# A delta-rule attention with a gated FFN on one core: the outputs' trip through DRAM by pairs of units, and another order of all tasks

## The chip, the cores and the metric

The kernel runs on one core of one Trainium2 chip. The time is the device time of one execution in microseconds (us). A core has five engines that run their own instruction queues in order: TensorE (PE, matrix products; PEld are its weight loads), VectorE (DVE), ScalarE (ACT), GpSimd (POOL) and SyncE (SP). SP computes nothing here: it issues the DMA transfers between DRAM and the core's memory, in the order of its own queue, and the issue of one takes it some 0.4 us. An engine whose next instruction has to wait holds up everything behind it in its queue.

## What is computed

For each of 4 batches and 8 heads, a state of 48 × 48 is carried along 768 tokens. Each token reads the state with its query, and then corrects it along its normalised key. The outputs of all heads, put side by side, are 3,072 rows of 384 features, which go through a gated two-layer network:

```python
for t in range(S):
    kt, vt, bt = (k_n[:, :, t], v[:, :, t], beta[:, :, t, None])
    y[:, :, t] = np.einsum('bhd,bhde->bhe', q[:, :, t], state)
    v_old = np.einsum('bhde,bhd->bhe', state, kt)
    state = state + bt[:, :, :, None] * np.einsum('bhd,bhe->bhde', kt, vt - v_old)
...
x = np.ascontiguousarray(attn_out.transpose(0, 2, 1, 3)).reshape(B * S, H * D)
h = x @ w_in          # 384 x 2048
g = h * np.cos(h)
return (g @ w_out)    # 2048 x 384
```

Everything is float32.

## The kernel before

**Units and pairs.** The 768 tokens are cut into 24 units of 32 tokens; a unit holds all batches and heads. Two units are a pair, and the network works on pairs, 2 × 128 rows each. The work of a unit n, by the names of the tasks in the code:

- `k`, `q`, `v`, from unit 8 on also `blocks`: loads, issued by SP (`load`, L294; `load_blocks`, L314). `turn` and `turn_out` turn keys and queries, on PE and ACT up to unit 7, on DVE from `blocks` afterwards.
- `gram` (PE, L545), `gram_keys` and `gram_queries` (DVE, L556 and L579): products of keys with keys and with queries.
- The triangular system of a pair m is inverted: `gram_put` of both units writes to DRAM (L597), `gram_get` reads it in another layout (L610, L618), `inv` runs column by column (L655, L662), on DVE for pair 0 and on POOL for all others, `put` writes the inverse (L676) and `get` reads it unit by unit (L687, L695).
- The path from unit to unit: `state` (PE, L712) applies the state, `right` (DVE, L727) makes the right-hand side, `solve` (PE, L775) applies the inverse (for units 0 and 1 in two halves, `solve_half` and `between`, L742), `solve_out` (DVE, L785), `update` (PE, L798) and `update_out` (DVE, L806) give the next state, `within` (PE, L815) completes the outputs.

**Outputs to features.** The network needs the outputs with features on the partitions. Units 0 to 3 are turned on PE (`features`, L834) and copied by ACT (`features_out`, L841). From unit 4 on DVE turns them in blocks of 32 × 32 (`within_turn`, L851), `within_put` (L861) writes them to a tile `y_dr` in DRAM, and `features_out`, by `features_move` (L868), reads them back into the pair's tile `x_ffn`. `y_dr` is made per unit, three at a time; its row of 1,536 bytes holds a partition's four batches side by side. The put therefore takes four DMAs a unit, one for each batch's 32 partitions, and the read takes one, in pieces of a whole row.

**Network.** The weights are 28 loads from DRAM (`weights`, L414), each followed by `split` on ACT, `shift` on DVE and `add` on POOL (L437). Pairs 0 and 1 take the first layer in plain form (`hidden`, L883), the others with fewer products (`layer`, L1000; sums of features by `x_sum`, L962). Then come four steps of gating, by turns on ACT and DVE (`turns` L923, `rest` L930, `cos` L939, `gate` L942), and the second layer, `out` (L1025 for pair 0, L1082 after), collected by ACT and DVE (L1119, L1132) and written by `store` (L1143). In a pair's first layer, `layer(p,0,0)` and `layer(p,0,1)` read only the first unit's features; later steps read the second unit's, or the sums.

**Order.** All tasks are registered with their engine and what they depend on, and are then emitted in an order written out by hand: `Order.LINE` (L53), a list of the tasks' numbers. So the order on each engine's queue is fixed, and a task also waits for the data that it uses. The costs and due times given to `add` are not used by this listing. Buffers are few: `x_ffn` has two, `y` one, and the one bank `two` serves `turn`, `gram`, `solve`, `update` and `features` in turn.

Of the kernel before, what the change touches and what calls it, by code (L numbers as in the profile page):

```python
# [10 lines left out]
FP = mybir.dt.float32  # L11
# [5 lines left out]
C = 32  # L17
# [36 lines left out]
0 1 2 3 4 5 6 1767 14 72 10 15 37 73 42 11 43 7 12 1771 16 38 13 75 17 96 39 40 44 45 18 46 20 48 99  # L54
1772 19 79 1775 50 80 76 77 49 97 47 1779 100 78 101 81 131 104 1773 132 1783 105 102 1768 1774 155
1780 106 51 82 52 107 1769 1784 53 134 1776 54 109 55 84 135 111 1781 1787 108 9 1777 1785 110 83
1778 1788 1782 1791 112 56 36 1770 113 22 41 138 1795 21 1789 23 139 24 25 26 136 27 114 1799 1796
28 1792 29 137 30 115 1786 32 186 31 140 1803 33 74 1807 57 1793 141 1794 1800 142 1790 34 35 1804
1797 1808 58 1805 1809 59 116 679 1810 60 61 818 62 1798 1811 1801 210 684 63 680 1815 681 241 64
1819 685 156 117 1802 65 1820 1812 8 66 686 687 67 1823 68 118 1813 689 143 159 187 1824 69 1816  # L60
1827 98 688 1825 119 1831 1817 86 160 161 162 164 682 163 1828 189 690 103 193 190 194 683 1814 85
1806 694 1832 1835 70 1818 691 71 87 88 165 692 1829 695 89 1839 699 166 1830 90 1836 92 133 1843
1821 191 1833 693 696 1837 697 91 700 1840 698 1822 701 192 704 702 93 705 709 703 1826 167 714 710
94 706 1841 719 265 95 1844 711 712 707 1834 243 1838 168 1847 708 715 169 1842 120 1851 195 731 121
196 1845 197 122 747 123 1846 713 1852 716 170 752 717 124 1848 125 244 718 748 735 1853 753 157
1855 211 1856 749 754 127 171 1849 126 1859 720 755 750 1854 757 1850 1857 128 1860 1861 756 129 758
762 732 751 130 763 214 759 760 215 767 296 1863 1864 158 764 216 765 1867 1858 172 145 761 217 1862
173 188 1868 1871 1865 174 721 1869 1866 768 736 766 769 1872 219 770 739 1873 1870 1875 146 772 771
198 247 1876 248 777 1877 778 1874 1878 245 782 779 249 722 773 144 220 218 147 774 723 221 148 269
819 222 725 737 724 780 149 223 268 151 726 822 152 150 175 820 740 823 176 727 270 775 781 320 783  # L70
741 298 776 224 212 177 728 153 178 729 743 784 733 785 246 787 786 179 788 351 299 790 180 182 821
793 183 794 791 154 744 181 225 792 746 796 184 798 250 200 789 730 799 242 251 800 252 213 801 201
745 797 185 271 253 802 272 273 804 827 303 828 826 742 734 806 829 226 274 227 830 842 228 843 300
276 831 229 803 832 833 824 807 275 844 199 808 835 834 836 837 277 805 838 839 202 845 840 846 847
848 795 203 302 266 849 809 850 204 206 851 205 207 841 854 810 231 230 375 811 323 852 304 853 855
858 232 738 825 233 859 856 860 862 278 301 234 353 208 861 235 812 863 857 873 236 814 324 874 875
305 237 864 238 865 866 815 306 406 279 209 868 867 890 876 325 869 307 870 877 239 280 354 813 326
881 281 357 878 282 255 816 240 879 871 882 308 889 327 880 883 329 884 892 267 872 885 921 358 328
922 920 923 895 896 886 887 888 893 283 924 925 936 926 331 927 256 898 929 284 330 332 891 900 937
894 938 254 930 901 928 257 355 333 897 285 931 902 258 259 359 903 334 378 817 430 932 335 940 261  # L80
904 939 933 941 942 906 262 260 943 908 286 297 899 287 934 935 408 944 288 952 461 948 909 945 289
263 321 946 356 949 947 379 910 905 953 336 950 290 291 911 954 337 338 409 956 912 360 292 984 913
951 907 413 412 264 955 957 293 294 380 914 967 958 968 969 916 917 959 918 361 960 322 962 961 964
963 362 983 970 971 972 986 973 915 381 382 975 976 310 965 977 295 974 989 384 383 1015 978 966 339
979 980 981 987 982 1016 990 1017 992 1014 985 919 994 988 1019 311 1018 995 996 1021 363 309 1030
312 1020 1022 433 434 313 1031 385 1023 1025 991 997 1024 485 1026 314 1034 386 316 315 998 1035
1000 1027 317 410 341 1036 1037 414 1002 387 1003 340 1032 1004 1028 463 1038 388 318 999 1039 411
1040 342 1005 1041 464 993 343 352 516 344 435 1033 389 1029 1006 1046 345 346 1001 467 1048 1042
1047 1043 1050 415 376 1044 1049 347 1061 1045 1062 1051 1078 1063 1052 1054 1007 348 1053 1055 1056
1064 1057 1065 1058 1008 390 416 1066 1059 377 1069 391 1070 417 1067 1010 1011 436 1068 1060 540  # L90
319 392 393 349 1012 365 1073 366 1077 1074 468 350 437 469 418 1009 394 1109 1071 1072 1080 1075
1083 1111 1108 1076 1081 1079 1110 1084 1086 1113 438 439 1115 364 1082 1112 1088 465 1089 367 441
1114 489 1090 1117 368 369 1124 1125 1013 488 440 1118 1126 523 1116 1091 371 407 1092 442 395 443
571 1094 370 1119 1127 1121 1120 1132 1096 1085 372 1128 1087 1133 1122 1097 1098 444 445 1134 1123
1135 1140 1129 1099 1093 373 1130 1136 396 1137 397 1138 431 1141 1100 1101 398 462 1139 1131 374
1142 518 446 1144 490 1146 519 399 466 1095 400 447 1145 1147 1102 1143 401 402 1155 1148 1150 403
1149 1151 1159 1160 522 1104 1156 1157 404 1105 1152 1106 1158 1103 1161 470 432 1163 471 1162 420
1164 405 520 1153 472 448 1171 421 1154 1165 491 1172 1203 595 1202 1166 473 1174 1167 1168 1205 521
1177 1169 1204 449 1175 1173 492 1206 1207 1170 1178 1209 494 1218 1208 1210 1211 493 1212 1176 1180
419 496 1219 1213 544 495 1214 1220 1222 573 1215 1182 1183 543 1223 1107 1184 1224 486 1221 1185  # L100
1226 422 1179 1227 450 1216 1228 1225 1186 497 423 1229 1234 424 426 1235 1236 574 1217 1230 1188
1231 425 1238 1232 498 1233 499 427 451 1237 1181 575 1190 1187 524 1191 1240 1266 452 1239 428 453
1249 517 429 1192 1250 1241 454 1193 455 457 1242 577 1244 1194 487 500 1243 1251 1195 458 501 1246
1245 1252 1196 1189 1257 1198 456 1253 459 578 626 502 1199 1247 1254 1200 1258 1259 545 460 1255
1260 1256 503 1265 1248 525 1261 1262 475 1268 526 1297 1299 1263 1298 1197 650 1296 579 504 1271
476 1269 1264 1301 1302 1201 528 576 1272 1274 1303 527 474 1300 1305 1304 1276 546 547 1307 1306
549 550 1309 1267 1320 1270 599 1308 548 1277 1321 477 505 478 1278 628 1322 1323 479 1279 481 1316
1312 1313 1317 1280 1310 482 551 480 598 552 1311 1314 1318 1282 1315 1319 506 1324 553 629 1328
1329 1284 507 1330 1332 1275 1333 508 554 1331 1285 1325 1343 509 1326 483 510 1327 1286 1273 1334
511 1336 580 512 484 541 1281 555 1335 1287 1283 1344 1288 513 542 1289 1345 556 1290 1338 1337 1292  # L110
514 633 1339 1293 581 1346 515 632 1347 1348 582 1360 1340 1351 1291 1294 600 1341 601 1352 1349 530
1353 602 583 1359 1354 1342 1362 604 1391 557 1390 1355 1356 1350 1363 1357 1392 1393 1358 558 1395
1397 1365 1396 1394 1398 531 1364 559 1399 1400 653 1406 529 603 1366 1407 605 1408 560 1401 1403
572 532 1409 1368 533 606 596 534 1402 1414 607 1370 536 1361 1415 1410 1416 1367 1417 1371 634 537
535 1372 1404 561 1411 1373 608 609 1295 630 597 1374 1412 562 1405 1376 538 1378 1375 563 1422 1379
1380 1369 564 1423 1418 1413 1377 1424 1454 539 610 1419 1381 565 631 654 567 1382 655 1426 1383 627
568 1420 566 1425 1437 1384 1421 635 636 569 585 611 1428 1427 1386 1385 570 1430 1387 637 1438 1429
1439 1432 1431 1440 1433 1388 1441 1434 1445 1442 1453 1435 1446 586 1447 1443 656 612 613 1448 1444
1455 1484 1436 1485 1456 1457 1487 1449 1486 657 1450 1459 1489 638 1460 1451 1452 1491 614 1458 659
1490 1488 584 1492 1500 1462 658 1493 1495 587 1501 1494 1497 1502 1464 1508 661 588 1496 1465 1466  # L120
1503 660 1389 1504 589 591 1505 1498 1509 1467 592 1468 1470 1506 1510 615 1511 651 590 662 1472
1461 1507 1499 616 663 1473 1474 1516 1512 1518 617 1517 1513 1548 1463 664 1469 618 1519 1531 1514
1520 1475 1476 1477 1515 1532 619 1522 1521 665 1533 620 1523 593 622 1524 1478 621 623 1526 594
# [1452 lines left out]
```

## Time and profile before

| what | value |
|---|---|
| runs of the kernel | 678.98, 673.96, 679.34 us; median 678.98 |
| profiled execution | 674.49 us, of which the span of its instructions 671.5 |
| granted TensorE clock, mean over the span | 0.992 |
| DVE, ACT, POOL busy | 70%, 33%, 52% |
| DMA engines | 57 MB by the hardware queue, 42.7% of 16 engines' span |
| `y_dr<-y` | 80 issues of 48 KB |
| `x_ffn<-y_dr` | 20 issues of 192 KB |

The profile is of one execution. Its page gives each engine's busy time, the span in 40 slices, the chain of work that ended last, and the costliest groups of instructions. Further views give the waits (which instruction waited for which, in total, how often, the longest), the timeline of one engine (start, duration, line, operation, tile, count), and the busy time of each engine in chosen stages (for PE, PEld, DVE, ACT, POOL, each with its count of instructions, then the granted clock, the DMA engines' busy share and GB/s). `L676` is line 676 of the kernel; `SPq` is SP's queue; `out<-in` names the tiles written and read.

### The profile page before, as it was taken

How to read it: one execution, taken by the hardware profiler on the slowest of the kernel's cores; microseconds unless marked ns; L12 is line 12 of the kernel's file. 1: busy time of each engine (PE TensorE's matmuls, PEld its weight loads, DVE VectorE, ACT ScalarE, POOL GpSimd, SP SyncE). 2: the span in 40 equal slices, each digit the busy share in tenths (PEclk: the TensorE clock that was granted, in tenths of full speed). 3: DMA queues.
4: the chain of work that ended last, by engine and by line, in shares of the span. 5: the costliest groups of instructions: out<-in, count | busy, mean ns of one | idle time of the engine just before them, and what ended most of it. 6: DMA issues, size and time to landing. Idle time of an engine off the chain costs nothing.

```text
span 671.5 us, 27694 instructions
## 1 busy us (share of the span) xinstructions
PE 611.3 (91%) x12060; PEld 573.7 (85%) x12060; DVE 468.4 (70%) x912; ACT 223.1 (33%) x376; POOL 348.0 (52%) x734
## 2 busy tenths in 40 slices
PE   4327789998999989999999999999999999999997
PEld 3216778885899879999899999999999999999997
DVE  6746676858877758668857876778695666667572
ACT  2424355541133222333323342242322423323330
POOL 4279867856868358318618648348286085000000
PEclk9999889999999989999999999999999999999999
DMA  8774784555463464453564454444632312101000
GB/s 175 168 174 114 165 188 102 124 104 100 98 105 60 93 110 68 87 100 66 102 107 79 80 98 78 86 85 74 118 72 62 80 27 54 40 19 44 1 24 23
DMA packets 230044, 59.66 MB, mean 89 GB/s; under 512 B 218916, under 2 KB 224820, under 8 KB 229924
## 3 DMA queue, kind: packets, MB, share of 16 engines
q1 hardware_dynamic: 226916, 57.03, 42.7%
q8 instruction: 94, 1.54, 1.0%
q10 hardware_dynamic: 2752, 0.43, 0.4%
q0 software_dynamic: 256, 0.44, 0.2%
q14 instruction: 26, 0.21, 0.1%
HBM read 43.17 MB, written 14.68 MB: 86 GB/s over the span
## 4 chain that ended last, share of the span: by engine, by line
PE 63%; POOL 11%; DMA 9%; SPq 7%; DVE 6%; issue 3%; ACT 1%; POOLq 0%; DVEq 0%; ACTq 0%
PE p_h L1000 25%; PE p_out L1082 24%; POOL part L655 4%; POOL z L662 4%; PE p_kq L712 3%; SPq L320 3%; PE p_u L775 2%; PE p_kq L815 2%; PE p_g L545 2%; PE p_s L798 2%; DMA kp<-in_k_dram 2%; PE p_o L1082 2%; DMA gb<-g_dr 1%; POOL w_in L437 1%; PE p_h L883 1%
## 5 line engine op out<-in xcount | busy, mean ns | idle before, releaser
L655 POOL TENSOR_TENSOR part<-z,gb 128x126 f32<-128x126 f32 (+22 forms) x341 | 136.8, 401 | 150.9 <-DMA gb<-g_dr 42.6
L662 POOL TENSOR_TENSOR z<-z,part 128x126 f32<-128x126 f32 (+22 forms) x341 | 138.0, 405 | 26.7
L1000 PE MATMUL p_h<-x_ffn,w_in 128*128 128x128 f32 x1120 | 144.9, 278 | 0.1
L1000 PEld LDWEIGHTS p_h<-x_ffn,w_in 128*128 128x128 f32 x1120 | 135.9, 193 | 1.8 <-DVE g_ffn L942 0.3
L923 ACT ACTIVATE turns<-p_h,quarter_turn 128x512 int32<-128x512 f32 x96 | 65.3, 685 | 174.7 <-DVE p_h L1018 112.8
L1082 PE MATMUL p_out<-w_out,g_ffn 128*128 128x192 f32 x672 | 121.6, 329 | 0.7 <-ACT o L1037 0.3
L1082 PEld LDWEIGHTS p_out<-w_out,g_ffn 128*128 128x128 f32 x672 | 107.8, 190 | 2.2 <-ACT o L1037 0.5
L939 ACT ACTIVATE turns<-turns,halfpi 128x512 f32<-128x512 f32 x96 | 68.2, 719 | 69.5 <-DVE turns L930 69.1
L1082 PE MATMUL p_out<-w_sum,g_ffn 128*128 128x192 f32 x496 | 89.6, 330 | 0.6 <-issue 0.5
L1082 PEld LDWEIGHTS p_out<-w_sum,g_ffn 128*128 128x128 f32 x496 | 80.1, 191 | 1.8 <-issue 0.4
L930 DVE SCALAR_TENSOR_TENSOR turns<-p_h,turns 128x512 f32<-128x512 f32 x96 | 65.2, 684 | 23.2 <-ACT turns L923 23.0
L942 DVE TENSOR_TENSOR g_ffn<-turns,p_h 128x512 f32<-128x512 f32 x96 | 64.7, 678 | 14.4 <-ACT turns L939 14.3
L1015 ACT COPY g_ffn<-p_h 128x512 f32<-128x512 f32 x60 | 34.8, 581 | 98.2 <-PE p_h L1000 98.2
L1018 DVE TENSOR_TENSOR p_h<-g_ffn,p_h 128x512 f32<-128x512 f32 x60 | 41.3, 689 | 30.7 <-PE p_h L1000 20.3
L1098 DVE TENSOR_TENSOR g_ffn<-g_ffn 128x512 f32<-128x512 f32 x88 | 61.7, 710 | 0.1
L883 PE MATMUL p_h<-x_ffn,w_in 128*128 128x128 f32 x384 | 47.7, 284 | 1.9 <-DVE g_ffn L942 1.9
L883 PEld LDWEIGHTS p_h<-x_ffn,w_in 128*128 128x128 f32 x384 | 46.1, 199 | 3.2 <-DVE g_ffn L942 1.2
L1132 DVE SCALAR_TENSOR_TENSOR o<-p_out,o 128x192 f32<-128x192 f32 x74 | 25.0, 351 | 30.9 <-PE p_out L1082 28.1
L1000 PE MATMUL p_h<-x_sum,in_sum 128*128 128x128 f32 x320 | 42.3, 277 | 0.9 <-DVE g_ffn L942 0.9
L466 POOL TENSOR_TENSOR knrm<-ksum,halves 128x16 f32<-128x16 f32 (+1 forms) x14 | 36.2, 2588 | 9.7 <-DVE ksum L454 8.8
L1000 PEld LDWEIGHTS p_h<-x_sum,in_sum 128*128 128x128 f32 x320 | 39.4, 192 | 1.4 <-PE p_h L1000 1.1
L785 DVE TENSOR_TENSOR u<-p_u,bz 128x384 f32<-128x384 f32 x48 | 24.4, 550 | 21.5 <-PE p_u L775 21.4
(111 smaller groups left out, 737.9 us busy)
## 6 DMA issues: line engine op xcount, KB each, us to landing
pairs<-in_moe_w_in_dram SPq DMA_DIRECT2D x12, 512.0 KB
pairs<-in_moe_w_out_dram SPq DMA_DIRECT2D x16, 384.0 KB
gb<-g_dr SPq DMA_DIRECT2D x22, 256.0 KB
vp<-in_v_dram SPq DMA_DIRECT2D x96, 48.0 KB
out_dram<-o SPq DMA_DIRECT2D x23, 192.0 KB
y_dr<-y SPq DMA_DIRECT2D x80, 48.0 KB
x_ffn<-y_dr SPq DMA_DIRECT2D x20, 192.0 KB
kp<-in_k_dram SPq DMA_DIRECT2D x128, 24.0 KB
```

Of the source, the lines that this page charges most:

```text
L466: nc.gpsimd.tensor_tensor(out=scales[m][2][:, part], in0=sums[m, part.start][:, 0:n], in1=halves[:, 0:n], op=ALU.pow,)
L655: eng.tensor_tensor(out=part, in0=z[:, 0:rows, j, None].to_broadcast(shape), in1=a[:, j, None, j + 1 :].to_broadcast(shape), op=ALU.mult,)
L662: eng.tensor_tensor(out=behind, in0=behind, in1=part, op=ALU.subtract)
L883: nc.tensor.matmul(p_h[:, i], w_in[:, t, (4 * k + i) * 128 : (4 * k + i + 1) * 128], moved(p, t, unit), start=(t == 0), stop=(t == KT - 1),)
L923: nc.scalar.activation(turns[p, f], hidden_of(p, f), AF.Identity, bias=quarter_turn, scale=TURN)
L930: nc.vector.scalar_tensor_tensor(out=r, in0=hidden_of(p, f), scalar=TURN, in1=t, op0=ALU.mult, op1=ALU.subtract,)
L939: nc.scalar.activation(r, r, AF.Sin, bias=halfpi, scale=2.0 * math.pi)
L942: nc.vector.tensor_tensor(out=place(p, f), in0=step_of(rests.pop((p, f)), f), in1=step_of(hidden_of(p, f), f), op=ALU.mult,)
L1000: nc.tensor.matmul(p_h[:, e], in_sum[:, odd_tile, 4 * s + e] if a == "s" else w_in[:, a, f * 128 : (f + 1) * 128], x_sums[p][:, unit] if b ...
L1018: nc.vector.tensor_tensor(out=block(p, s, 0, 1) if i == 3 else p_h, in0=block(p, s, *one), in1=p_h, op=ALU.add,)
L1082: nc.tensor.matmul(p_o, left(p, part, a)[:, e % 4], right(e, b), start=(e == 0), stop=(e == FT // 2 - 1), skip_group_check=True,)
L1098: nc.vector.tensor_tensor(out=left(p, s, to), in0=left(p, s, one), in1=left(p, s, two), op=op)
```

## The change

Three parts. The tile `y_dr` is made per pair, as [4 quarters of the features, 2 units, 128 rows, 96]: `within_put` writes a unit in one DMA over 128 partitions, in pieces of 384 bytes, and `features_move` reads a pair in four DMAs, one for each 32 partitions of `x_ffn`, in pieces of 384 bytes, for both units at once. The task `features_out` exists once a pair, for its odd unit, and depends on both units' puts; the ten even ones are gone (1,879 tasks become 1,869, which shifts the numbers). And all tasks have another order. In it, on SP's queue:

- from the start on: `weights 0`, `k 2`, `weights 1`, `q 2`, `gram_put 0`, `gram_put 1`, `weights 2`, `k 3`, `gram_get 0`, `weights 3`, `q 3`, `k 4`, `weights 4`, `v 0`, `k 5`, `weights 5`, `put 0`, `v 1`, `weights 6`, `gram_put 3`, `q 4`, `gram_put 2`, `weights 7`, `get 0`, `weights 8`, `gram_get 1`. Before it was `weights 0`, `k 2`, `q 2`, `weights 1`, `k 3`, `gram_put 0`, `gram_put 1`, `weights 2`, `gram_get 0`, `q 3`, `weights 3`, `k 4`, `q 4`, `weights 4`, `k 5`, `gram_put 3`, `gram_put 2`, `weights 5`, `v 0`, `gram_get 1`, `weights 6`, `put 0`, `v 1`, `weights 7`, `get 0`;
- the read of pair 2 follows directly on `within_put 5`; at pair 3 a `store` and `v 11` stand between, at pair 5 half of `blocks 16` and a `store`, at pairs 4, 6 and 7 a `store`.

On PE, `turn 4` comes after `within 0` rather than before `solve_half 0`, `hidden(0,2)` between `solve_half 1` and `between 1`, `hidden(0,4)` and `features 1` between `gram 5` and `turn 6`, `solve 4` before `hidden(1,14)` and `out(0,0,3)` rather than after them, and `layer(2,0,0)` after the first product of pair 1's second layer rather than after the fourth. The last fourteen `out` tasks, all of pair 11, stand as they did. On DVE the parts of pair 0's inverse stand in a row; on POOL eight weight additions, rather than three, come before the first part of pair 1's inverse, and four rather than eight between the parts of pair 2's.

```diff
@@ -51,90 +51,89 @@
     LINE = """
-0 1 2 3 4 5 6 1767 14 72 10 15 37 73 42 11 43 7 12 1771 16 38 13 75 17 96 39 40 44 45 18 46 20 48 99
-1772 19 79 1775 50 80 76 77 49 97 47 1779 100 78 101 81 131 104 1773 132 1783 105 102 1768 1774 155
-1780 106 51 82 52 107 1769 1784 53 134 1776 54 109 55 84 135 111 1781 1787 108 9 1777 1785 110 83
-1778 1788 1782 1791 112 56 36 1770 113 22 41 138 1795 21 1789 23 139 24 25 26 136 27 114 1799 1796
...
+0 1 2 3 4 5 6 1757 72 10 37 14 11 7 12 42 38 1761 39 13 15 40 16 43 17 44 1758 18 45 46 19 75 73 20
+48 1765 50 79 96 49 1769 97 47 76 1759 77 80 104 78 99 131 51 1762 81 105 52 53 54 1773 9 154 55
+1777 82 100 56 1770 36 1766 1778 1763 1771 134 101 1760 102 106 107 1774 135 41 1781 1772 108 1767
+83 136 22 1782 109 1783 23 1775 1764 132 84 1785 1779 21 1789 1784 110 1793 1786 1768 1780 1776 24
...
 """
...
@@ -853,21 +852,23 @@
             p_kqs.pop(n)[:, :, 1].rearrange("p a j e -> p j a e"),
         )
 
+    y_drs = {}
+
     def within_put(n):
-        y = ys[n]
-        ys[n] = dram.tile([128, B, KT * C], FP, name="y_dr")
-        dst = ys[n].rearrange("(z i) b c -> b i z c", i=C)
-        for b in range(B):
+        if n % 2 == 0:
+            y_drs[n // 2] = dram.tile([4, 2, B * C, KT * C], FP, name="y_dr")
+        nc.sync.dma_start(
+            out=y_drs[n // 2][:, n % 2].rearrange("z p c -> p z c"),
+            in_=ys.pop(n).rearrange("p (z k) t -> p z (k t)", k=KT),
+        )
+
+    def features_move(m):
+        x = xts[m] = ffn_pool.tile([128, 2, B, KT, C], FP, name="x_ffn")
+        src = y_drs.pop(m).rearrange("z u (b i) c -> z i (u b) c", i=C)
+        for z in range(4):
             nc.sync.dma_start(
-                out=dst[b], in_=y[quarter(b)].rearrange("i (z k) t -> i z (k t)", k=KT)
-            )
-
-    def features_move(n):
-        if n % 2 == 0:
-            xts[n // 2] = ffn_pool.tile([128, 2, B, KT, C], FP, name="x_ffn")
-        nc.sync.dma_start(
-            out=xts[n // 2][:, n % 2].rearrange("p b k t -> p b (k t)"), in_=ys.pop(n)
-        )
+                out=x[quarter(z)].rearrange("p u b k t -> p (u b) (k t)"), in_=src[z]
+            )
 
 
 
@@ -1308,10 +1309,11 @@
             add(("within_turn", n), "DVE", 0.5, lambda: within_turn(n), [("within", n)],
                 makes=[("y", ("y", n))], uses=[("p_kq", n)])
             add(("within_put", n), "SP", 0.45, lambda: within_put(n), [("within_turn", n)],
-                makes=[("y_dr", ("y_dr", n))], uses=[("y", n)], moves=1.0)
-            add(("features_out", n), "SP", 1.8, lambda: features_move(n),
-                [("within_put", n)] + ([("features_out", n - 1)] if second else []),
-                makes=[] if second else [("x", ("x", m))], uses=[("y_dr", n)], moves=1.0)
+                makes=[] if second else [("y_dr", ("y_dr", m))], uses=[("y", n)], moves=1.0)
+            if second:
+                add(("features_out", n), "SP", 1.8, lambda: features_move(m),
+                    [("within_put", n - 1), ("within_put", n)],
+                    makes=[("x", ("x", m))], uses=[("y_dr", m)], moves=1.0)
             return
         add(("within_out", n), "ACT", 0.52, lambda: within_out(n), [("within", n)],
             makes=[("y", ("y", n))], uses=[("p_kq", n)])
```

## The prediction

> **What bounds the kernel now.** I read the page's busy row and slices first, then the busy time by stage, then who TensorE (PE) waited for, and last the order of the sync queue (SP), on which all the edited transfers are issued.
>
> ```profile
> span 671.5 us, 27694 instructions
> PE 611.3 (91%) x12060; PEld 573.7 (85%) x12060; DVE 468.4 (70%) x912; ACT 223.1 (33%) x376; POOL 348.0 (52%) x734
> PE   4327789998999989999999999999999999999997
> ```
>
> PE is the engine of the span, so the change can only act on the 671.5 − 611.3 = 60.2 us in which PE is idle. The stages say where those lie (columns: stage, its length, busy time of PE and so on):
>
> ```profile
> 0.00:61.00 61.00, 23.96 (x648) 19.49 (x648) 35.83 (x111) 21.55 (x40) 32.86 (x52) 1.00 0.73 164
> 61.00:100.00 39.00, 31.27 (x911) 28.99 (x912) 28.08 (x45) 18.69 (x36) 30.69 (x45) 0.91 0.71 163
> 200.00:240.00 40.00, 36.95 (x848) 34.56 (x845) 30.73 (x59) 13.53 (x22) 20.95 (x53) 1.00 0.51 91
> 345.00:645.00 300.00, 300.00 (x5542) 290.06 (x5541) 212.42 (x402) 98.43 (x159) 132.09 (x313) 1.00 0.34 65
> ```
>
> 37 us are lost before 61 us, 7.7 in the next stage, a few in each stage up to 345, and nothing at all from 345 to 645. So an edit of a path that runs to the end is worth only what it does early. The waits of PE, from three windows (up to 61 us, 61 to 135, 135 to 360; total, times, longest):
>
> ```profile
> PE p_t L514 <- DVE tt L579: 11.9, 1, 11.9
> PE p_w L742 <- DMA halves_z<-z_dr: 6.6, 2, 6.3
> ...
> PE p_w L742 <- DVE rhs L727: 2.2, 1, 2.2
> ...
> PE p_u L775 <- DMA zt<-z_dr: 2.6, 2, 1.9
> PE p_u L775 <- DVE tt L579: 2.2, 1, 2.2
> ```
>
> The early loss ends with the first solve, which starts at 48.13 when unit 0's inverse has come back through DRAM. That return is set by SP's order (start, duration, line, transfer):
>
> ```profile
> 37.02 0.40 SPq L676 DMA_DIRECT2D z_dr<-z  x1
> 37.46 5.94 SPq L309 DMA_DIRECT2D vp<-in_v_dram  x4
> 44.04 3.92 SPq L687 DMA_DIRECT2D halves_z<-z_dr  x4
> ...
> 221.83 1.81 SPq L861 DMA_DIRECT2D y_dr<-y  x4
> 226.95 1.37 SPq L868 DMA_DIRECT2D x_ffn<-y_dr  x1
> ```
>
> Later SP hardly rests: from 199.73 to 262 us its pieces follow each other within about a microsecond, and the outputs of unit 7, transposed by 216.89, are put at 221.83.
>
> **The trip through DRAM.** A pair issues 8 puts and 2 reads now. A put takes 0.43 us and 0.05 to the next, a read 0.37 and 0.05: 8 × 0.48 + 2 × 0.42 = 4.7 us of SP a pair. Afterwards it is 2 puts (one 128-partition issue; the row nearest to it, z_dr at L676, takes 0.40) and 4 reads (like the 4-issue rows at 0.48): 2.8 us. Saved: 1.9 us a pair, 19 over ten pairs. PE doesn't wait for SP's time as such, though, and part is given back: the pair's read now waits for the second put to land (some 2.2 us: unit 15's last put ends at 462.94, its read starts at 465.17), and in the new order only a store (0.6) stands between the two at pairs 4, 6 and 7, nothing at pair 2. The loads queued behind that read wait too. I take a net 0.8 us of SP a pair.
>
> The path from the last product of a pair to its first layer is now: transpose 0.57 (L851), put 0.45, landing 2.2, four reads 1.9, landing 2.4 (the z reads landed 2.72 and 1.92 after their last issue in the chain, the x_ffn read itself 3.31): 7.5 to 8.4, I take 8.0. There is a new wait in it. Today `layer(p,0,0)` and `(p,0,1)` read only the first unit's half: at 227.85 PE starts layers of pair 3 while the second half's read was issued at 226.95 and lands 3.31 later. Each new read fills a quarter of the partitions for both units, so the first layer waits for all four. Behind it on PE's queue stands everything. The cover is the PE work between `within(2p+1)` and `layer(p,0,0)` in the new order. Counted with 0.89 for a layer's product, 1.30 an `out` part, 1.31 a `state`, 0.8 to 0.85 for `gram`, `solve`, `update`, `within`, it is 10.7, 13.5, 13.1, 14.4 and 11.4 us for pairs 2 to 6 (pair 3: two layers of one product and two of two, 5.3; four `out` parts, 5.2; two grams and a state, 2.9). That leaves 2.7, 5.5, 5.1, 6.4 and 3.4 us for SP to be late. In the trace SP put the second units' outputs 2.5, 4.9, 3.6, 5.4 and 0.7 late: just inside. I add 2 us for this, between 0 and the 16.6 of the slower rival below.
>
> The pieces read shrink from 1,536 to 384 bytes. The row: the z reads come in pieces of 128 bytes and landed no later than the x_ffn read, so I charge nothing. The Trainium skill ("DMA: Bandwidth & Descriptors", Specifications) asks for 512 bytes or more for line rate, and speaks against this part of the change; no run here shows 384-byte reads. If that halved the rate, the rival on small pieces below is what would follow.
>
> **The order at the start.** `put 0` first. Between `gram_get 0` (issued until 20.42) and `put 0` stand 12 SP tasks now, 7 in the new order: q3, k4, v0, k5 at 2.0 and three weights at 0.45, so SP is there at 29.8. `k 3`, moved ahead of `gram_get 0`, takes 1.9 us in the time (17.50 to 19.26) in which SP waits for the fold to land anyway. The inverse on DVE ran from 23.04 to 32.62 with two `gram_keys` and a shift between its parts; in a row its parts take 7.2 us, so to 30.2. Its copy on ACT, which came at 35.24 behind a split and a square, comes next after `turn_out 3`: put at about 30.7, not 37.02. Then `get 0` has v1, q4, two gram_puts and two weights ahead (6.0 us) in place of v1 and one weight: 37 us, or 41 if v1's four issues again take 5.94 where others take 1.93. With 4.1 us to land (44.04 to 48.13) the first solve starts between 41 and 45; the bad end is 48, if queued weights hold it up. I take 44, as the slow v1 is a row: −4.1. `turn 4` (2.1), done in the idle time before, now runs behind the solve, and covers a gap of 0.98: +1.1. Sum −3.0, ends −6 and +1.
>
> From 61 to 135: PE's 2.21 before `solve_half 1` goes (`right 1` gets 1.5 us more cover), the 0.61 before `between 1` goes under `hidden(0,2)`, and of the 1.74 before `turn 6` some 1.0 goes under `hidden(0,4)`; what is late next is features 1's copy on ACT, which the same bank waits for. −3.8, ends 0 and −6.
>
> `solve 4` waited 2.16: inverse 2 on POOL has four weight additions (1.02 each) between its parts in the new order, eight now, so it returns some 4 us sooner. `solve 4` itself stands 5.3 PE-us earlier, which the earlier lead covers: −2, ends 0 and −2.2.
>
> From 160 to 345 PE loses 6.3 us in eight gaps, 3.6 of them with SP or a z read just before. I take −2, ends 0 and −6. After 345 nothing can be gained, and the last fourteen `out` tasks are the same: 0.
>
> Sum: −3.0 − 3.8 − 2 − 2 + 2 = −8.8. The profiled execution took 674.49 (3.0 more than its span), so 665.7. The median of the three runs, 678.98, is 4.5 above it; runs of one kernel lie that far apart here, so I put the median of the new one 2 above: 668.
>
> **Rivals.** *Small pieces land late.* If the four reads take twice the 3.31 us of the x_ffn row, the path is 3.3 longer, and with the lateness above pairs 2 to 6 stall 3.1, 2.7, 1.8, 2.3 and 0.6: 10.5 us in place of my 2. 665.7 + 8.5 = 674, as fast as the profiled run. For it: the row has one landing only, DMA engines are half busy until 345. Against: the z reads. 0.2.
>
> *SP stays late, slower.* In the trace SP put the first units' outputs 10.2, 8.7, 8.1, 5.0 and 6.3 us late. If the second units' puts, moved among other loads, meet that, the new whole-pair wait costs 7.5, 3.2, 3.0, 0 and 2.9: 16.6 us. If also the lead of the start isn't kept by SP (the −2 and −2 above gone), 674.5 − 6.8 + 16.6 = 684, 686 on the median's scale. It decides from about 5 us of lateness at `within_put 5, 7, 9`. Against: SP has 1.9 us less to do a pair, and `put 2`, which held it until 139.5, comes sooner. 0.2.
>
> *The start gives nothing:* DMA engines are 73% busy in the first stage, weights ahead of `get 0` keep it at 48, and what follows shifts with it. −8.8 + 3.0 + 2 = −3.8: 671, 673 on the median's scale. 0.15.
>
> **The numbers.** The forecast, 668, has 0.45; its own range is 660 to 674, from the ends of the terms. About 1% (6.8 us) can be told from no change, so faster is below 672.2 and slower above 685.8. Faster: 0.42 of the forecast, 0.03 of the small pieces, 0.07 of the third rival: 0.52. Slower: 0.12 of the second, and 0.06 for stalls that I haven't found: 0.18. The rest, 0.30, is within. The range for 8 in 10 goes from 658 to 686.
>
> **What would show it.** The first `p_w` (L742) at about 44, and PE idle before 61 us some 3 lower; no 2.2 before L742 and none before L775 near 150; PE still never idle after 345; 20 puts and 40 reads; the first layer of each pair starting without a gap. A gap before L1000 behind `x_ffn<-y_dr` at pairs 2 to 6 would speak for the first two rivals (the landing or the queue's lateness tells which), `p_w` at 48 for the third. More PE time in a term that I set to zero, after 345 above all, would make the prediction wrong.

## The result, and the profile after

The changed kernel took 671.03 us (median of 8 runs, 669.73 to 673.52), the kernel before 677.21 in the same session (8 runs, 673.96 to 679.35). The ratio is 0.9916, 95% interval [0.9888, 0.9943]: a gain of 0.8%, which by the prediction's bound of 1% counts as no change. (671.03 lies below 672.2, which the prediction named as the bound of faster, but the kernel before took 677.21 here and not 678.98, so the ratio decides.) Measured twice more, the unchanged new kernel gave 0.9938 [0.9905, 0.9972] and 0.9921 [0.9894, 0.9948].

The first profiled execution of the new kernel was the slowest of its eight runs (673.52 us), so it lies hardly below the profiled run of before. A second profile of the same kernel has a span of 667.2 us, a third 669.8. Gains of a few us are therefore read from medians; the profiles serve to find places.

The page of the new kernel: span, busy row, transfers (issues, KB each):

```profile
span 671.7 us, 27640 instructions
...
PE 607.6 (90%) x12060; PEld 571.4 (85%) x12060; DVE 466.9 (70%) x912; ACT 223.6 (33%) x376; POOL 343.5 (51%) x734
...
y_dr<-y SPq DMA_DIRECT2D x20, 192.0 KB
x_ffn<-y_dr SPq DMA_DIRECT2D x40, 96.0 KB
```

20 writes and 40 reads, as the change says. The stages of the first profile (columns as before):

```profile
0.00:61.00 61.00, 22.22 (x584) 18.39 (x584) 40.41 (x111) 20.89 (x38) 32.74 (x47) 0.64 0.83 181
61.00:100.00 39.00, 26.80 (x795) 24.39 (x794) 18.15 (x34) 18.28 (x35) 25.48 (x46) 0.87 0.58 129
...
240.00:345.00 105.00, 104.95 (x2187) 100.67 (x2162) 77.88 (x147) 31.44 (x51) 54.79 (x132) 1.00 0.49 86
345.00:645.00 300.00, 297.19 (x5515) 286.79 (x5514) 211.41 (x399) 97.61 (x157) 131.36 (x309) 1.00 0.33 63
```

(The clock column of the first stage, 0.64 here and 1.00 before, marks no difference in speed: the 64 products of `between 0` take 1.50 us in both, at 48.37 here and at 51.32 before.)

Three things differ from what was forecast. PE idles 38.8 us before 61, where it idled 37.0. It idles 12.2 us in the next stage, where it idled 7.7. And in the 300 us in which it never idled before it now idles 2.8. From 240 to 345 nothing is lost any more. The waits of the new kernel say what these are (PE; windows up to 61 us, 61 to 135, 360 to the end):

```profile
PE p_w L741 <- DMA halves_z<-z_dr: 16.1, 1, 16.1
...
PE p_u L774 <- issue: 2.9, 1, 2.9
...
PE p_g L544 <- ACT kq_t L523: 4.7, 1, 4.7
PE p_kq L711 <- issue: 2.3, 1, 2.3
...
PE p_t L513 <- ACT x_ffn L840: 0.8, 1, 0.8
...
PE p_kq L711 <- issue: 2.1, 2, 1.4
PE p_h L1001 <- issue: 0.7, 1, 0.7
```

(L741 is the L742 of before, L774 the L775, L711 the L712, L544 the L545, L1001 the L1000.) The 2.2 us before `solve_half 1` and the 2.2 before `solve 4` are gone. In their place stand a wait of 4.7 us for ACT, and waits called "issue", inside groups of equal products, in which PE waited for nobody.

Less idle time is not what the profiles show, though. PE idles 60.2 us before, and 64.1, 60.2 and 59.9 in the three profiles of the changed kernel; its busy time fell, from 611.3 to 607.6, 607.1 and 609.9. A part of that is the clock. In the profile of before, PE waits 1.88 us until 240.48, the granted clock is 0.50 from 241.1 to 244.5, and eight products of a layer take twice the 1.05 us that they take at 491.07:

```profile
242.06 2.08 PE L1000 MATMUL p_h<-x_ffn,w_in 128*128 128x128 f32 x8
```

PE's busy time in stretches with that clock, from 61 us on, adds up to 9.9 us before, and to 6.5, 4.2 and 9.7 in the three profiles. The rest of the fall was not traced.

**The start** went as worked out, on SP's queue:

```profile
30.73 0.39 SPq L675 DMA_DIRECT2D z_dr<-z  x1
31.17 4.00 SPq L308 DMA_DIRECT2D vp<-in_v_dram  x4
...
36.78 3.65 SPq L308 DMA_DIRECT2D qp<-in_q_dram  x4
...
41.60 1.87 SPq L686 DMA_DIRECT2D halves_z<-z_dr  x4
```

`put 0` at 30.73 (30.7 was forecast), `get 0` at 41.60 (41), and the first solve at 45.35 (44, from 48.13). That `get 0` comes so near the 41 is partly luck: `v 1` took 4.00 us rather than the 5.94 of that estimate, and `q 4` 3.65 rather than 1.93.

**The new wait.** ACT, and then PE, around 85 us (start, duration; in brackets the idle time before and who ended it):

```profile
85.88 0.84 ACT L448 ACTIVATE ksq<-kp 128x768 f32<-128x768 f32 x1 [5.82 <-POOL w_in L436]
...
87.24 1.05 ACT L523 COPY kq_t<-p_t 128x512 f32<-128x512 f32 x2
```

```profile
83.24 0.37 PE L711 MATMUL p_kq<-st,kq_t 48*32 48x48 f32 x23 [2.26 <-issue]
88.34 1.18 PE L544 MATMUL p_g<-kq_t 48*32 48x64 f32 x64 [4.73 <-ACT kq_t L523]
89.45 5.49 PE L884 MATMUL p_h<-x_ffn,w_in 128*128 128x128 f32 x24
```

The new order puts `square 3` (ACT squares pair 3's keys, L448) ahead of `turn_out 5`, the copy that `gram 5` waits for; before, `turn_out 5` came first. `square 3` needs one of the eight buffers of tag "g", which the weights share, and none is free until POOL has done a weight addition (L436). POOL does it when the inverse of pair 1 is through, at 84.6, and that inverse began late: eight additions go ahead of it, and its `gram_get 1` is issued at 44.46. So a square that nobody needs soon holds ACT for 5.8 us and PE for 4.7. The granted clock is then 0.50, from 84.6 to 94.8, and `hidden(0,4)` takes 5.49 us, where the same 24 products take 2.94 elsewhere in this trace.

### The profile page after: what moved, and what is told of

It is laid out like the page before. It is cut to its first block, busy times and chain, and to the rows that moved or that the text cites. A ratio compares the mean times of both kernels' runs of the same rounds, so it can differ in the third digit from the quotient of the medians.

```text
span 671.7 us, 27640 instructions
## 1 busy us (share of the span) xinstructions
PE 607.6 (90%) x12060; PEld 571.4 (85%) x12060; DVE 466.9 (70%) x912; ACT 223.6 (33%) x376; POOL 343.5 (51%) x734
## 3 DMA queue, kind: packets, MB, share of 16 engines
q8 instruction: 94, 1.54, 1.0%
## 4 chain that ended last, share of the span: by engine, by line
PE 83%; DMA 4%; DVE 3%; issue 3%; POOL 3%; SPq 3%; ACT 1%; ACTq 0%; DVEq 0%; POOLq 0%
PE p_h L1001 29%; PE p_out L1083 29%; PE p_h L884 6%; PE p_kq L711 4%; PE p_s L797 3%; PE p_u L774 3%; PE p_kq L814 3%; PE p_out L1026 2%; PE p_g L544 2%; PE p_o L1083 2%; SPq L308 1%; DMA qp<-in_q_dram 1%; POOL knrm L465 1%; DMA x_ffn<-y_dr 1%; POOL z L661 1%
## 5 line engine op out<-in xcount | busy, mean ns | idle before, releaser
L654 POOL TENSOR_TENSOR part<-z,gb 128x126 f32<-128x126 f32 (+22 forms) x341 | 133.2, 391 | 107.9 <-DMA gb<-g_dr 52.6
L1001 PE MATMUL p_h<-x_ffn,w_in 128*128 128x128 f32 x1120 | 143.2, 276 | 0.7 <-issue 0.7
L1001 PEld LDWEIGHTS p_h<-x_ffn,w_in 128*128 128x128 f32 x1120 | 135.4, 192 | 1.9 <-issue 0.9
L1001 PE MATMUL p_h<-x_sum,in_sum 128*128 128x128 f32 x320 | 41.6, 277 | 0.0
L1001 PEld LDWEIGHTS p_h<-x_sum,in_sum 128*128 128x128 f32 x320 | 38.8, 192 | 0.6
```

The lines of the kernel that those rows point to most:

```text
L654: eng.tensor_tensor(out=part, in0=z[:, 0:rows, j, None].to_broadcast(shape), in1=a[:, j, None, j + 1 :].to_broadcast(shape), op=ALU.mult,)
L1001: nc.tensor.matmul(p_h[:, e], in_sum[:, odd_tile, 4 * s + e] if a == "s" else w_in[:, a, f * 128 : (f + 1) * 128], x_sums[p][:, unit] if b ...
```

## Experiments

Ratios are to the kernel before, from the runs of the same session (its medians: 675.43 for the first four rows, 672.54 for the next four, 675.41 for the last four); times are comparable within a session. A second measure places a lead within the kernel: the start of a pair's first layer product against its start in the profile of before, corrected for the PE work that the order has moved past it (by the prediction's durations 7.8 us less ahead of pair 2 in the new order, at most 1.3 later on). Negative is earlier; one profile each.

| kernel | median us | ratio, interval | pair 2 | pair 4 | pair 6 | pair 8 | pair 10 | last `out` |
|---|---|---|---|---|---|---|---|---|
| after_again | 670.46 | 0.9938 [0.9905, 0.9972] | −0.4 | −5.4 | −7.6 | −7.0 | −5.6 | −4.2 |
| layout_only | 673.7 | 0.9968 [0.9937, 0.9999] | +3.1 | +0.9 | +0.2 | +0.2 | +0.3 | +0.3 |
| order_only | 673.11 | 0.9959 [0.9929, 0.9989] | +1.5 | −4.1 | −4.0 | −3.1 | −2.0 | −1.4 |
| early_new | 671.27 | 0.995 [0.9918, 0.9982] | +3.4 | −4.3 | −5.3 | −5.2 | −5.1 | −5.1 |
| late_new | 673.07 | 1.0004 [0.9978, 1.0029] | −0.1 | −3.4 | −5.7 | −5.7 | −4.5 | −2.9 |
| square_later | 666.17 | 0.9895 [0.9867, 0.9924] | −2.5 | −7.1 | −9.4 | −8.8 | −7.6 | −6.3 |
| split_reads | 665.74 | 0.9907 [0.9871, 0.9943] | −0.1 | −3.3 | −4.7 | −4.3 | −3.9 | −3.8 |
| split_reads16 | 690.37 | 1.0248 [1.021, 1.0286] | −2.5 | −4.1 | +4.0 | +9.3 | +12.9 | +14.1 |
| after_third | 670.66 | 0.9921 [0.9894, 0.9948] | +1.8 | −3.0 | −5.1 | −4.0 | −2.5 | −1.6 |
| square_again | 668.07 | 0.9895 [0.9862, 0.9929] | −1.0 | −4.9 | −7.0 | −5.9 | −4.4 | −3.1 |
| get_early | 669.94 | 0.9926 [0.9892, 0.996] | −0.6 | −5.1 | −7.0 | −6.1 | −4.6 | −3.3 |
| square_old_trip | 670.42 | 0.9929 [0.9903, 0.9955] | +4.7 | −2.5 | −3.7 | −3.0 | −1.2 | −0.7 |

### Which part does it

*after_again* is the changed kernel as it is. *layout_only* has its trip through DRAM, in the order of before:

```diff
 # the changed kernel's code; LINE as before the change, less the ten tasks
-features_out(4) features_out(6) ... features_out(22)
```

*order_only* is the reverse:

```diff
 # the code of before; LINE as after the change, with the even units' reads put back
+features_out(n)      # n = 4, 6, ..., 22
 within_put(n + 1)
```

*early_new* follows the new order up to `layer(2,0,0)` and the old one from there, *late_new* the other way round; both have the new trip.

> The changed kernel once more, for a second profile and a closer ratio. If the stalls inside groups of PE's small products (2.9 us at 54.8, 2.3 at 83.2, 13 us in all in the first profile) belong to that one execution, they are gone or elsewhere here and the span is near 668.5; if they belong to the program, they come back at the same products. The 4.7 us before gram 5, which ACT's turn_out 5 ended, should come back either way, since ACT stands before it at the square of pair 3, which waits for a buffer that POOL frees. Ratio to before 0.989 to 0.994.

> The order of before with the new trip: the ten even reads are taken out of the list, all else keeps its place. If the order makes the gain and the trip next to nothing, the ratio to before is 0.998 to 1.002, PE idle before 61 us stays at 37, and from 160 to 345 it stays within 2 us of 6.3. If fewer issues on SP make the gain, it is 0.994 or lower, with the loss in 160 to 345 gone. If the wait of a pair's first layer for both units, or the 384-byte pieces, cost, it is above 1.003, with gaps before the layers behind x_ffn<-y_dr at pairs 2 to 6.

> The new order with the old trip; the ten even reads are put in just before the put of the pair's odd unit, where the old order has them too. If the order makes the gain, the ratio to before is 0.989 to 0.995. If the trip makes it, 0.998 or higher; with SP's 1.9 us a pair more to do, gaps before p_u behind zt<-z_dr should then come back in 160 to 345.

> The new trip, with the new order up to the first layer of pair 2 and the old order of what is left. If the gain is made by the start of the order (first solve some 3 us sooner, solve 4 sooner) and kept, the ratio is 0.988 to 0.994, as with the whole new order. If it is made after 180 us, the ratio is that of the new trip with the old order.

> The mirror of the mixed order: the old order up to the first layer of pair 2, the new one after it, with the new trip. If the order's gain lies at the start, the ratio is that of the new trip with the old order, 0.996 to 0.999, and the layers of pair 2 start at 185 to 188 us. If it lies after 180 us, 0.992 to 0.995.

The gain is small and spread: the layout alone gives 0.3%, the order alone 0.4%, both 0.6%, and the intervals overlap. With the new order only behind pair 2 nothing is left to be measured (1.0004); with it only ahead of pair 2, 0.5% is.

In the landmarks the changed kernel is hardly ahead at pair 2, in any of three profiles (+5.1 in the first, −0.4, +1.8). It gains 7 to 9 us from there to pair 6, and gives back some 3.5 afterwards. That is the opposite of the forecast, which had 8.8 us of gain ahead of pair 2 and none on balance behind it.

PE's idle time, which needs no correction, says the same. Up to the start of pair 2's layers it is 49.5 us before, and 55.6, 51.3 and 51.6 in the three profiles of the changed kernel. From there to the start of pair 6's layers it is 6.2 before and 1.0, 1.7 and 1.2 (*layout_only* 4.4, *early_new* 0.8, *late_new* 2.4). From there to the end it is 4.6 before and 7.5, 7.2 and 7.1.

In *layout_only* the wait of a whole pair's reads is seen once (PE):

```profile
229.74 2.47 PE L1001 MATMUL p_h<-x_ffn,w_in 128*128 128x128 f32 x20 [0.66 <-DMA x_ffn<-y_dr]
```

In the new order no first layer waits for its features. The packets' records say that the small pieces are on the whole no later: in *after_again* the reads in 384-byte pieces end 1.3 to 2.5 us after the last issue (one 3.2), half of them within 1.4; in the profile of before the reads in 1,536-byte pieces end after 1.4 to 2.1, half within 1.75. A 384-byte packet took 24 ns on the mean, one of 1,536 bytes 88: four times the bytes in 3.7 times the time. The prediction weighed a rule of the Trainium skill ("DMA: Bandwidth & Descriptors", Specifications: 512 bytes or more for line rate). No loss from it shows in these numbers.

### The wait at `square 3`

*square_later* moves it, and the sum that DVE makes of it, behind the work that is due:

```diff
 # ACT
 cos(0,2)
-square(3)
 cos(0,0)
 turn_out(5)
 split(15) split(14) split(13) turns(0,4) features_out(1) cos(0,4)
+square(3)
 # DVE
 shift(14)
-sum(3)
 gate(0,0) shift(13) shift(16) shift(12) gate(0,4)
+sum(3)
```

*square_again* is the same kernel, and *after_third* the unchanged new one, on one chip in a later session.

> The changed kernel with two tasks moved: the square of pair 3's keys (ACT) and its sum (DVE) come after the gating of hidden(0,4), not before turn_out 5. If the 4.6 us before gram 5 are ACT waiting at that square for a buffer, they are gone, hidden(0,4) starts near 81 us instead of 88, at full clock, and hidden(0,6) is set by POOL's additions 9 and 10, near 89 instead of 94.6. If the start still decides the end, the ratio to before falls to 0.985 to 0.990; if what follows is set by POOL and SP anyway, it stays at 0.992 to 0.996 and the lead is gone again by the first layer of pair 2.

> The changed order with square 3 moved behind cos(0,4) on ACT and sum 3 behind gate(0,4) on DVE, once more, now on the same chip as the changed kernel. If the wait for the g buffer at square 3 costs the end of the kernel what it costs at hidden(0,4), it is 3 to 5 us faster than the changed kernel of the same call. Rival: the lead is eaten before the stretch without gaps, and the two differ by less than 1.5 us.

> The changed kernel as it is, beside the three others on one chip. Its median lies 0.6 to 0.9% under the kernel before; the wait of about 4.6 us before gram 5 and the half clock behind it recur.

PE in *square_later*:

```profile
81.85 0.37 PE L711 MATMUL p_kq<-st,kq_t 48*32 48x48 f32 x23 [2.26 <-issue]
...
82.84 4.57 PE L884 MATMUL p_h<-x_ffn,w_in 128*128 128x128 f32 x24
```

The 4.6 us before `gram 5` are gone, and `hidden(0,6)` starts at 89.5, 5.1 earlier than in *after_again*. In the paired runs 668.07 stands against 670.66: 2.6 us, half of it, and less than the 3 to 5 expected. The profile of *square_again* shows where some of it went: PE waits 2.33 us at 106.34 for DVE's `solve_out 2`, a wait that *after_third* hasn't got. What was ahead at pair 2 by 2.8 is still ahead by 1.5 at the last `out`. The measured ratio (0.9895 in both sessions) is the best of all kernels here, but its interval overlaps those of the others. And in the session of *square_later* (666.17) the changed kernel was not run; *split_reads*, the next experiment, has `square 3` where the change put it, took 665.74 in that session, and has the wait in its profile:

```profile
87.29 1.18 PE L544 MATMUL p_g<-kq_t 48*32 48x64 f32 x64 [7.36 <-ACT kq_t L523]
```

So it is shown that the edit takes the wait away; that the kernel ends sooner by it rests on the medians of one session.

### Is it SP's time?

*split_reads* reads a pair in eight transfers, as much SP time as before the change, *split_reads16* in sixteen; all else is the changed kernel.

```diff
-        for z in range(4):
-            ... out=x[quarter(z)] ..., in_=src[z]
+        for u in range(2):
+            for z in range(4):
+                ... out=x[quarter(z), u] ..., in_=src[z, :, B * u : B * u + B]
```

> The changed kernel with eight reads a pair, four for each unit, in place of four: SP issues 10 DMAs a pair, as before the change, and the first layer of a pair can start on the first unit's half again. If the saved 1.9 us of SP a pair is what the trip gains, the ratio to before rises by 0.002 to 0.004 against the changed kernel, to 0.996 to 0.998. If the gain of the trip is elsewhere (one put for four), it stays within 0.001 of it.

> Sixteen reads a pair, 5.8 us more of SP a pair than with four. If SP's time is on the path between 160 and 345 us, five pairs of it cost some 10 to 25 us, a ratio of 1.01 to 1.03, with gaps before p_u behind zt<-z_dr and before the layers. If it is hidden behind PE's work, the ratio stays below 0.998.

Four more issues a pair (1.9 us of SP) cost nothing that can be measured: 0.9907, among the three ratios of the changed kernel. Twelve more (5.8 us), in reads of 24 KB each, cost over 3%: 1.0248. *split_reads16* is level with the others to pair 4 and then loses at every pair. Its stage from 345 on, and the first of PE's waits from 200 to 360:

```profile
345.00:645.00 300.00, 294.03 (x5583) 281.44 (x5582) 207.97 (x391) 92.90 (x149) 135.18 (x314) 0.99 0.34 66
```

```profile
PE p_u L774 <- DMA zt<-z_dr: 4.5, 9, 1.5
```

The inverses' reads, queued on SP behind the features' reads, arrive late. By these two kernels SP's slack a pair lies between 1.9 and 5.8 us, and 1.9 us within it is worth nothing that can be measured. Whether the smaller reads of *split_reads16* cost something besides SP's time was not tested.

*square_old_trip* asks the same from the other side: *square_later* with the old trip (four writes a unit, even reads put back as in *order_only*).

> As square_again, but with the old trip: y_dr per unit, four writes a unit and one read, each even unit's read directly ahead of the odd unit's write on SP. Theory that the new layout as such is worth little: within 3 us of square_again. Rival, that the SP time it saves carries the lead of the order: 4 us or more slower than square_again, with gaps before p_u behind zt<-z_dr after 200 us.

670.42 against 668.07: by the medians the trip is worth 2.4 us with the better order, though the intervals of the ratios overlap. A place where the two profiles differ is the write of unit 4, on SP, and what stood behind it, on DVE:

```profile
156.14 3.46 SPq L861 DMA_DIRECT2D y_dr<-y  x4
159.64 1.93 SPq L309 DMA_DIRECT2D vp<-in_v_dram  x4
```

```profile
164.81 0.96 DVE L502 TENSOR_TENSOR vp<-vp,knrm 128x768 f32<-128x768 f32 x1 [6.61 <-DMA kp<-in_k_dram]
```

Four writes hold SP from 156.14 to 159.60, the load of `v` (L309) is issued behind them, DVE stands 6.6 us in front of the instruction that scales it, and PE then waits 4.0 us before `update` (167.98). (The view names the next load on SP, of keys; by the semaphores the last parts of `v` landed at 164.4 and 164.6.) In *square_again* this `v` is issued at 154.39, and DVE waits 0.7. Other profiles don't bear out the size: in *order_only*, where the same four writes start at 155.95 and take 1.82 us, DVE waits 2.9 there and PE 0.4; in the first profile of the changed kernel, with one write, DVE waits 3.5 and PE 1.5. So the four writes delay this load, but how much of the 2.4 us is theirs is not shown. *split_reads* has as many issues as the old trip, none of them ahead of this load, and DVE waits 2.5 there and PE not at all. That the place of an issue counts for more than the sum of SP's time fits all of this, and stays argued.

### The first solve, six us sooner

*get_early* is *square_later* with `get 0` directly behind `v 1`:

```diff
 # the order of the transfers
 put(0) v(1)
+get(0)
 weights(6) gram_put(3) q(4) gram_put(2) weights(7)
-get(0)
 weights(8)
```

> As square_again, with get 0 moved on SP's queue from behind weights 7 to directly behind v 1, so that weights 6, gram_put 3, q 4, gram_put 2 and weights 7 come 1.9 us later. The inverse's write lands at about 33, get 0 can be issued at 35.4 and not 41.5: the first p_w at about 39, 6 us sooner than square_again. Theory that the first solve binds what follows: 4 to 6 us of that are left at pair 2's first layer, and the time is 4 to 6 us under square_again. Rival: POOL's inverse of pair 1, which does not move and ends at about 84, and the weight splits set the stage from 80 to 110; then hidden(0,6) starts within 2 us of square_again's 89.5 and the time is within 2 us of it.

669.94 us, not faster than *square_again*. The first solve started at 44.11, 2.0 earlier and not 6. The inverse's data had landed at 39.3 by the packets' records. ACT, DVE and PE:

```profile
35.72 1.78 ACTq L686 DMA_DIRECT2D halves_z<-z_dr  x4
37.54 0.66 ACT L421 ACTIVATE w_in<-pairs 128x512 f32<-128x512 f32 x1 [6.84 <-DMA halves_z<-z_dr]
```

```profile
40.59 0.95 DVE L453 TENSOR_REDUCE ksum<-ksq 128x16 f32<-128x768 f32 x1 [5.11 <-ACT ksq L448]
...
43.59 0.41 DVE L578 TENSOR_TENSOR tt<-p_g,consts 128x256 f32<-128x256 f32 x1
```

```profile
44.11 1.83 PE L741 MATMUL p_w<-vp,halves_z 32*32 32x48 f32 x64 [14.94 <-DMA g_dr<-g]
50.22 1.50 PE L741 MATMUL p_v<-u_half,halves_z 32*32 32x48 f32 x64 [4.28 <-ACT u_half L751]
```

Half of the transfers of `get` are issued by ACT (L686). They were moved past four splits and a square on ACT's queue, and ACT computed nothing for 6.8 us, until the inverse had landed in DRAM and its reads were issued. So DVE got the squared keys late and was done with the products of `gram 3` and `gram 2` only at 44.0, and `gram 2` holds the bank `two` that the solve writes to. (The view names a DMA write as releaser of the solve; by the semaphores `get` had landed by 39.7, and DVE's was raised at 44.02, 0.1 us before the solve.) Then PE lost 4.3 us more before `between 0`, waiting for a copy on ACT that by the same view waited for a buffer that POOL's additions free. The test says little on what a sooner first solve is worth; it shows that the solve has several conditions within a few us, and that moving one of them moves another.

### The waits called "issue"

No run was made for these; they are read from the traces. In the profile of before, PE's waits of over a quarter of a us without a releaser sum up to 1.6 us from 48 us on, in *layout_only* to 1.3. In the three profiles of the changed kernel it is 13.0, 9.8 and 7.8, in *order_only* 10.7, *square_later* 7.6, *split_reads* 3.9, *split_reads16* 0.8. They recur at the same product, as here in the first profile of the changed kernel, and in the second (1.16 us before the same 19 products, at 488.25):

```profile
493.03 0.36 PE L711 MATMUL p_kq<-st,kq_t 48*32 48x48 f32 x19 [1.43 <-issue]
```

The page counts transfers of a kind of their own:

```profile
q8 instruction: 94, 1.54, 1.0%
```

94 transfers of 16,384 bytes: 1.54 MB for PE's 24,283 instructions (products, weight loads and 163 of its sequencer), 64 bytes each, so one transfer holds 256. Counting PE's instructions from 0, the one that follows such a wait, where it is over 0.5 us, is number 961, 1473, 2241, 2497, 5825, 6081, 7361, 14273, 19137 and 22977 in the first profile: each leaves a remainder of 193 on division by 256. In all fourteen profiles there are 66 waits of this kind over 0.5 us from 48 us on, and 65 of them have this remainder, those of before among them; the one other is 1.2 us long, in *order_only*. Each of the 65 ends 1.2 to 1.8 us after such a transfer has ended. The reading that fits this is that PE had run out of instructions at a block's edge and waited for the next block.

The Trainium skill ("Runtime: NRT & Kernel Launch", Instruction fetch mechanics) describes blocks of 16 KiB with 256 instructions, fetched while the current ones run, and calls the cost of crossing an edge mostly hidden. The size agrees with this trace. That it is hidden holds for the order of before (1.6 us); in the new order up to 13 us show. Why nearly the same order shows 3.9 us in one kernel and 13.0 in another was not found.

## Why the prediction was right or wrong

It said 668, and 671.03 came: inside the range, with half the gain. The outcome to which it gave the highest chance, faster (0.52), did not come; no change, which came, had 0.30. Its premise, that the change can only act on the time in which PE is idle, did not hold in the profiles (60.2 us idle before, 59.9 to 64.1 after, and 1.4 to 4.2 less busy). By its own steps:

- **First solve, −4.1.** Right in mechanism and nearly in size: −2.8. Of the 1.4 us missing, 0.6 are `get 0`, at 41.60 and not at 41 (`q 4` took 3.65 where 1.93 was assumed, and `v 1` less than was allowed for it); the rest lies in the landing. But the indicator named for it, PE idle before 61 us some 3 lower, failed: idle time rose by 1.7. A wait of 2.9 us at a block's edge, inside `solve 0`, took the lead back; in the second profile it is 1.8, and a lead of 1.1 is left at `within 0`.
- **61 to 135 us, −3.8.** This step failed: PE idles 9.7 us there before, and 12.6, 11.8 and 11.9 in the three profiles after. The three waits named did go, and what was named as late next, the copy of `features 1` before `turn 6`, is what is left there (0.8). But only PE's queue was followed. ACT's queue had changed too: `square 3` ahead of `turn_out 5`, and in front of it a buffer that POOL frees. It costs 4.7 us of waiting and some 2.5 for the low clock. *square_later* shows it: without it the stage from 61 to 100 idles 7.2 us rather than 12.2. That is as much as before (7.7), so even then nothing is left of the 3.8: the block edge of 2.26 stays. At the end of the kernel the edit is worth 2.6 us by the medians of one session; in the other, *split_reads*, which has the wait, ends as soon.
- **Solve 4, −2.** The wait is gone, as forecast.
- **160 to 345, −2 (0 to −6).** Inside its range, and mostly too small: PE idles 6.7 us there before, and 4.4, 2.5 and 1.2 after; from 240 to 345 it loses 0.05 where it lost 2.5. But two of the eight gaps that were counted (0.54 at 301.60, 1.02 at 327.59) lie at block edges and had nothing to do with SP. The landmarks from pair 2 to pair 6 gain more, 7.2 in *after_again*; they hold the time at half clock too. *early_new* and *late_new* gain as much there (8.7 and 5.6): the place was right, but neither the new order of this part nor a lead at its start is needed for it.
- **The new wait for a pair's features, +2 (0 to 16.6).** None in the new order, 0.66 once in the old. The 2.2 us for the put's landing were misread: four loads (462.98 to 465.00) stood on SP between that put and its read. With nothing between them, at pair 2, the read is issued 1.9 us after the put's issue in the first profile (172.72, 170.81) and 3.5 in the second (169.68, 166.14). Both rivals that lived on it fell. *Small pieces land late*: they don't. *SP stays late*: the second units' outputs are put within 0.03 us of their transposition at pairs 2 to 4 (169.90, 219.42, 267.06) and 1.3 late at pair 5. *split_reads16* shows that a loss of this kind exists, with twelve more issues a pair than this change makes.
- **After 345, 0.** Wrong, and the sentence that named this as the danger was right: PE idles 2.8 us there in the first profile, and the landmarks lose 3.4 from pair 6 on in *after_again*; of the 2.8 lost after pair 8, two block edges (1.16 and 1.19) make up 2.35.
- **SP's 1.9 us a pair.** Rightly not counted as PE's time. The 0.8 net of it shows nowhere that these runs resolve, unless at unit 4's write.
- ***The start gives nothing*** forecast 671 for the profiled execution and 673 for the median, which came out between that and the forecast's 668. Its mechanism, weights that keep the first solve at 48, did not happen; that its sum is about as near is luck, as other waits took the start's gain.

The stretch from pair 2 to pair 6 recovers in nearly every variant, *layout_only* included (from +3.1 to +0.2), as far as PE's idle time there, 6.2 us before, is gone (0.8 to 4.4 left in them, 8.8 in *split_reads16*, which recovers nothing). What remains open: which part of the change takes away which of these waits, why PE's busy time fell, and what decides whether a block of instructions comes late.

## What to carry to other kernels

When an order is changed, walk each engine's queue, not just that of the engine that sets the time: an early task that nobody needs soon can stand in front of a due one and wait for a buffer (`square 3`), and a transfer issued from a computing engine's queue can hold that engine until its source is there (`get 0`, 6.8 us of ACT). Where SP is nearly full, look also at which transfer stands ahead of a load that is due, and not only at the total of issues. And groups of small products use up a block of 256 instructions fast (the 128 products of `state 1` and their weight loads in 1.4 us, at 61.06 in the first profile): waits inside a group of equal products, with no releaser, are looked for at steps of 256 instructions.

## What the runs showed of the hardware

- PE waits at its instruction blocks' edges, by the reading above: up to 2.9 us each, 7.8 to 13 us in an execution of the changed kernel, 1.6 before; none had been expected.
- Behind some waits the granted clock is 0.50 for a while: the 24 products of `hidden(0,4)` took 5.49 us behind waits of 2.26 and 4.73, 4.57 behind 2.26 alone (*square_later*), 2.94 in *get_early*, where 0.47 was lost just before. It is not so behind every wait: in *late_new* PE waits 2.32 us until 168.88, and the clock stays at 1.00.
- Four loads' issues on SP took 1.9 us in some places and 3.65 to 5.94 in others, among them right behind the `put` of pair 0's inverse (5.94 before, 4.00 after); the cause was not looked into.
